# Batched stages of a recurrent-attention layer reordered, and two buffers of its chain exchanged

## The chip, the cores and the metric

The kernel runs on one core of a Trainium2 chip. The metric is the device time of one execution in microseconds (us). The engines of a core work side by side, each through its own list of instructions in order: TensorE (PE, matrix products, with the loads of its weights listed as PEld), VectorE (DVE), ScalarE (ACT), GpSimd (POOL) and SyncE (SP, which here issues transfers only). Transfers (DMAs) are issued by SP, ACT and POOL and carried out by 16 DMA engines.

## The reference

Input and output are a sequence of 2048 tokens of 640 features, bf16. Four layers run one after the other, A, B, A, B, each on the normalized result of the one before and added to it. Layer A is the one that the change touches:

```python
mem = mem0                              # 8 rows of 640
for s in range(64):                     # 64 segments of 32 tokens
    h = concat([mem, xs[s]])            # 40 rows
    q, k, v = h @ Wq, h @ Wk, h @ Wv    # 32 heads of 192
    p = softmax(mask(q @ k.T * 192 ** -0.5))
    o = (p @ v) @ Wo
    mem = o[:8]                         # memory of the next segment
    outs.append(o[8:])
x = x + concat(outs)
```

The mask lets the 8 memory rows see all 40 rows; the 32 tokens see the memory and the tokens up to themselves. Since the memory of a segment is made by the segment before it, the 64 segments are a serial chain. Layer B is a linear attention over the whole sequence.

## The kernel before

**The two stages of a layer A.** Each segment has 40 rows. The kernel takes 32 of them through the chain (8 memory rows and the first 24 tokens) and computes the keys and queries of the last 8 tokens of each segment, the border tokens, for all 64 segments in a batch ahead of it. The batched stage is `A_pre` (from L836), the chain `A_chain` (from L1033). Both write out their order of instructions by hand: each engine runs its list in the order of the code, and a step that waits holds up all that is behind it on its engine.

**Rounds and weights.** The 32 heads go in four rounds r of 8 heads. A matrix Wq, Wk or Wv has five pieces of 384 KB for each round. Some pieces stay in SBUF for the whole layer, the others share slots and are streamed again for each segment (`load_slot`, L748). Half of the output weights of two rounds shares one place in the same way (`load_piece`, L797). A streamed load is held back until a named step of PE (table `PACE`, L26, function `release`), and then goes out on SP's queue.

**`A_pre`.** The segments are worked in two halves h of 32. A step (h, r) computes keys and queries of one round for one half: 120 products at L998, evicted in turn by DVE (L94) and ACT (L96) into one of two staging buffers, and stored to `kqb` in DRAM by a transfer on ACT's queue (L1015). In layer 0 the steps alternate over the halves, rounds 3, 2, 1, 0. In layer 2 half 0 runs through rounds 0 to 3, then half 1 through 3 to 0. Each step issues the loads of its own weights (`load_matrix`, L755 or L748), and layer 0 those of the next round too. `first_values` computes the border values of the first eight segments for a round (L257) and stores them to `vb` (L261). In layer 0 the stage also normalizes all rows as tasks between evictions, and lays the output weights out anew in DRAM, `wo_rows`: 32 transfers of 240 KB on SP (`lay_out_wo`, L816), 16 of them after step (0, 1) and 16 after (0, 0). Parts of them are fetched into SBUF (`early_wo`, `late_wo`, L774). The first 32 rows of the chain, `first_rows`, come by a transfer on SP at L1014.

**`A_chain`.** Each segment runs four rounds n = 0 to 3, every other segment in the reverse order of r. A round projects Q, K and V (L1129), computes scores (L1166), applies exp on ACT (L1247), weights the values (L1179), scales the result on ACT (L1209), turns it on DVE (L1350 for rounds 0 and 2, L1358 for 1 and 3) and multiplies with the output weights into `ps_w` (L1237). For each round POOL fetches the border keys and queries (`kqb`, L1098, three buffers, four turns ahead), copies them into place (L1105) and fetches the border values (`Vp<-vb`, L1109).

The border values themselves are made in the chain for a group of eight segments ahead: at the end of each segment one unit is computed from the tokens `tT` (L257, `next_values`), evicted by ACT at the start of the next segment into `vt` (L1276), and stored to `vb` by SP (L261). The tokens of a new group are loaded by POOL (L247) in two halves through one place `xt`, and turned by DVE (L250), in 6 segments of each layer.

**Who shares which place.** `vt` holds the border values on their way to `vb`, and then the turned rows of round 0 in the same segment. `ots` holds the turned tail rows of the segment before (`otb`) on their way to DRAM, then the turned rows of round 1, then `xt`. The tail rows of the segment's first two rounds go to the second half of `vt` at n = 2.

```python
if n == 0:
    rows = self.two_heads(vt).rearrange("p e (c j) -> p e c j", j=64)
```

Of the kernel before, what the change touches and what calls it, by code (L numbers as in the profile page):

```python
# [122 lines left out]
class Kernel:  # L123
# [139 lines left out]
    def kept_tokens(self):  # L263
        return self.under[:, self.ot_at:self.ot_at + 320].rearrange("p (b t) -> p b t", b=self.KC)
# [571 lines left out]
    def A_pre(self, xn_dram, li, load_matrix, piece, wo_mid, wo_end, lay_out_wo, early_wo, x_raw):  # L836
# [11 lines left out]
        vts = [wo_end[:, 2 * VH * i:2 * VH * i + 2 * VH] for i in range(2 * NR)]  # L848
        with ExitStack() as es:
# [14 lines left out]
            def gather(dst, src, h, k, queues=None):  # L864
                xv = src.rearrange("(s t) d -> t s d", t=32)
                for t2 in range(TP):
                    e = queues[t2 % 2] if queues else nc.gpsimd if k % 2 else nc.scalar
                    e.dma_start(out=dst[SH * t2:SH * t2 + SH, :], in_=xv[24 + TP * k + t2, SH * h:SH * h + SH])
# [54 lines left out]
            def all_rows():  # L923
                rows = [slice(P * b, P * b + P) for b in range(self.NB)]
                t = in_turn([norm_tasks(lambda x, q=q: nc.gpsimd.dma_start(out=x[:], in_=x_raw[q, :]),
                                        lambda xn, q=q: nc.gpsimd.dma_start(out=xn_dram[q, :], in_=xn[:]))
                             for q in rows])
                return [f for i in range(0, len(t), 4) for f in (*t[i:i + 4], None)]

            def keep_tokens(k):  # L930
                nc.gpsimd.tensor_copy(out=self.kept_tokens().rearrange("p b (t s) -> p b t s", s=8),
                                      in_=columns(0).rearrange("p b (t s) -> p b t s", s=SH)[:, :, :, 8 * k:8 * k + 8])

            def first_values(r):
                for G in range(2):
                    ps = ps_.tile([P, 512], F32, name="ps_pre", tag="bank")
                    self.tail_values(ps, lambda i: self.kept_tokens()[:, i, :], r, G, piece)
# [20 lines left out]
            if x_raw is not None:  # L958
# [3 lines left out]
            seen = set()  # L962
            for h, ri, r in steps:
                if h not in seen and (x_raw is None or h == 0):
                    seen.add(h)
                    xBT = columns(h)
                    for k in range(NT):
                        if x_raw is not None:
                            xb = normed[h, k]
                        else:  # L970
                            xb = xB[h][k % 2]
                            gather(xb, xn_dram, h, k)
                        transpose_rows(xb, h, k)
                        if x_raw is not None:
                            busy(3)
                xBT = columns(h)
                if turn == 0:
                    keep_tokens(0)
                st = sts[turn % 2]
                turn += 1  # L980
                if h == 0 and ri == 1:
                    self.build_A_consts()
                if x_raw is not None and (h, ri) == (0, 0):
                    for h1 in range(1, NH):
                        tasks += tails(h1)
                if x_raw is not None and (h, ri) == (NH - 1, 0):
                    tasks += all_rows()
                if x_raw is not None and h == NH - 1 and ri == NR - 1:
                    early_wo(True)
                for mi, m in enumerate("KQ"):  # L990
                    load_matrix(m, r)
# [24 lines left out]
                if x_raw is not None and (h, ri) == (0, 0):  # L1016
                    for h1 in range(1, NH):
                        for k1 in range(NT):
                            transpose_rows(normed[h1, k1], h1, k1)
                if h == 0:  # L1020
                    first_values(r)
                if h == 0 and ri == NR - 1:
                    keep_tokens(1)
                if h == NH - 1 and ri == 1 and x_raw is None:
                    load_matrix("V", 0)
                    early_wo(True)
                if h == NH - 1 and ri == NR - 1:
                    early_wo(False)
# [4 lines left out]
    def A_chain(self, xn_dram, at_dram, li, load_slot, piece, late_wo, load_both, wo, low):  # L1033
# [3 lines left out]
        with tc.tile_pool(name=f"A{li}_ch", reuse_waits="tile", bufs=1) as sp, \  # L1037
# [264 lines left out]
            for s in range(NSEG):  # L1302
# [64 lines left out]
                for n in range(L):  # L1367
# [36 lines left out]
                    if n == 1:  # L1404
                        turn_tails(s, 1)
# [127 lines left out]
```

## Time and profile before

| | us |
|---|---|
| median of 3 runs | 3296.66 |
| lowest and highest | 3291.12, 3306.54 |
| the profiled execution | 3315.67 |
| its span from first to last instruction | 3313.9 |
| PE busy in it | 3038.2 |
| granted TensorE clock in it | 0.987 |

Stages of the profiled execution, from the starts and ends of instructions in its timeline:

| stage | from | to |
|---|---|---|
| layer 0, batched stage | 0 | 157.7 |
| layer 0, first segment of the chain | 157.7 | 199.6 |
| layer 2, batched stage | 1687.7 | 1812.7 |
| layer 2, first segment of the chain | 1812.7 | 1840.9 |

Rows are read like this. A group or timeline row names the line of the kernel, the engine, the operation, and out<-in by the program's names; `x20` counts instructions. `[0.64 <-DVE under L1350]` is idle time of that engine just before, and what ended it. A waits row reads: engine, what waited, what it waited for, then the total in us, the number of times and the longest. A row of the chain of waits has start, duration and what was running or under way. `under` is the SBUF tensor in which `vt`, `ots` and others lie, `arena` the large one with weights. SPq is a transfer issued by SP.

### The profile page before, as it was taken

The page shows a single profiled execution, that of the slowest core. Times are in us where ns is not written, and L with a number is a line of the kernel's source. Part 1 is how long each engine was busy: PE and PEld are TensorE (multiplying, and loading weights), DVE is VectorE, ACT ScalarE, POOL GpSimd, SP SyncE. Part 2 cuts the span into 40 slices and gives each one's busy share as a digit, 9 for nine tenths or more (in the row PEclk, how much of TensorE's full clock was granted, in tenths as well). Part 3 has the DMA queues.
Part 4 walks back from the last instruction along what each step waited for, and adds up shares of the span by engine and source line. Part 5 has one row for each costly group of instructions (what it writes and reads, how often), then busy time and mean ns, then how long its engine had stood idle before and what let it go on. Part 6 is the DMA issues. An engine that isn't in the chain of part 4 may idle for free.

```text
span 3313.9 us, 141368 instructions
## 1 busy us (share of the span) xinstructions
PE 3038.2 (92%) x59586; PEld 1926.3 (58%) x59586; DVE 2170.0 (65%) x5425; ACT 1897.0 (57%) x4537; POOL 1379.5 (42%) x2852
## 2 busy tenths in 40 slices
PE   7879999999999999999999899999999999998999
PEld 5745565565555555555468555565556655555553
DVE  4557677777767667746653676667766766776565
ACT  2346666666666666646443566666666666665463
POOL 1244544545444545431121554545454554454300
PEclk8989999999999999999999999999999999999999
DMA  9787777777777777760277777777777777777400
GB/s 342 276 284 250 232 246 250 244 238 254 247 230 239 248 249 230 253 236 9 94 256 257 260 254 238 232 237 250 249 233 244 254 241 231 247 257 262 164 1 32
DMA packets 338812, 749.66 MB, mean 226 GB/s; under 512 B 68538, under 2 KB 115378, under 8 KB 335106
## 3 DMA queue, kind: packets, MB, share of 16 engines
q1 hardware_dynamic: 268258, 637.09, 56.6%
q0 software_dynamic: 66848, 77.71, 8.7%
q10 hardware_dynamic: 3072, 25.82, 2.0%
q8 instruction: 469, 7.68, 0.9%
q14 instruction: 165, 1.35, 0.1%
HBM read 670.77 MB, written 78.01 MB: 226 GB/s over the span
## 4 chain that ended last, share of the span: by engine, by line
PE 48%; DMA 35%; DVE 7%; ACT 5%; issue 4%; SPq 1%; POOL 0%; DVEq 0%; POOLq 0%; ACTq 0%
DMA vb<-under 12%; DMA arena<-in_A_Wv_dram 11%; PE ps_w L1237 9%; PE ps_qk_k L1129 6%; PE ps_v L1129 6%; PE ps_qk_q L1129 5%; DMA Vp<-vb 3%; PE ps_s L1166 3%; PE kv L1488 2%; PE ps_x L257 2%; PE ps_pre L998 2%; PE ps_o L1179 2%; DMA arena<-wo_rows 2%; PE ps_wo L466 2%; PE ps_pq L517 1%
## 5 line engine op out<-in xcount | busy, mean ns | idle before, releaser
L1129 PEld LDWEIGHTS <-hT 128*32 128x32 bf16 x30720 | 795.2, 97 | 511.1 <-DVE hT L1437 77.2
L1149 DVE STREAM_TRANSPOSE QK<-raws 128x512 bf16<-128x512 bf16 (+1 forms) x1152 | 712.4, 634 | 131.3 <-ACT raws L1144 103.9
L1129 PE MATMUL ps_qk_q<-arena,hT 128*32 128x384 bf16 x10240 | 509.3, 327 | 47.7 <-DVE hT L1437 23.8
L1129 PE MATMUL ps_qk_k<-arena,hT 128*32 128x384 bf16 x10240 | 513.6, 328 | 7.9 <-DMA arena<-in_A_Wk_dram 7.1
L1105 POOL COPY QK<-kqb 64x192 bf16<-64x192 bf16 x1024 | 349.6, 341 | 325.1 <-PE ps_s L1166 286.1
L1109 POOL DMA_DIRECT2D Vp<-vb x512 | 258.1, 504 | 537.5 <-PE ps_t L1192 302.3
L1129 PE MATMUL ps_v<-arena,hT 128*32 128x384 bf16 x8192 | 440.1, 327 | 28.2 <-DMA arena<-in_A_Wv_dram 20.7
L1144 ACT ACTIVATE raws<-ps_qk_k 128x512 bf16<-128x512 f32 (+1 forms) x640 | 313.6, 510 | 220.7 <-PE ps_qk_k L1129 218.7
L1209 ACT ACTIVATE raws<-ps_o,under 128x192 bf16<-128x192 f32 x1024 | 373.6, 420 | 111.0 <-DVE under L1203 104.5
L1144 ACT ACTIVATE raws<-ps_qk_q 128x512 bf16<-128x512 f32 x512 | 304.7, 595 | 230.8 <-DVE under L1350 136.6
L1237 PE MATMUL ps_w<-arena,under 128*32 128x320 bf16 x6144 | 307.8, 301 | 77.1 <-DVE under L1350 57.5
L1158 DVE CAST Vp<-ps_v 64x384 bf16<-64x384 f32 x512 | 286.4, 559 | 51.4 <-ACT Vp L1156 36.9
L1098 POOL DMA_DIRECT2D kqb<-kqb x512 | 287.1, 561 | 73.0 <-POOL QK L1105 59.4
L1166 PEld LDWEIGHTS <-QK 128*80 128x80 bf16 x4096 | 195.4, 120 | 158.6 <-issue 157.0
L1156 ACT ACTIVATE Vp<-ps_v 64x384 bf16<-64x384 f32 x512 | 246.4, 481 | 68.3 <-PE ps_v L1129 66.0
L1166 PE MATMUL ps_s<-QK 128*80 128x80 bf16 x4096 | 252.4, 209 | 2.6 <-PE ps_v L1129 0.7
L1094 POOL DMA_DIRECT2D attn<-under x128 | 91.2, 713 | 360.5 <-DVE under L1090 329.5
L1247 ACT ACTIVATE E<-ps_s 80x320 bf16<-80x320 f32 x512 | 217.6, 425 | 29.3 <-PE ps_t L1192 28.5
L1237 PEld LDWEIGHTS <-under 128*32 128x32 bf16 x6144 | 149.7, 96 | 115.9 <-DVE under L1350 70.6
L998 PEld LDWEIGHTS <-arena 128*128 128x128 bf16 x1920 | 190.8, 100 | 43.5 <-issue 10.7
L1276 ACT ACTIVATE under<-ps_x 128x384 bf16<-128x384 f32 x112 | 55.1, 492 | 264.9 <-PE ps_x L257 264.9
L1179 PE MATMUL ps_o<-Vp,E 80*32 80x193 bf16 x4096 | 179.7, 249 | 22.7 <-DMA Vp<-vb 10.8
(165 smaller groups left out, 4378.3 us busy)
## 6 DMA issues: line engine op xcount, KB each, us to landing
arena<-wo_rows SPq DMA_DIRECT2D x560, 320.0 KB, 5.9
arena<-in_A_Wq_dram SPq DMA_DIRECT2D x427, 384.0 KB, 6.1
arena<-in_A_Wk_dram SPq DMA_DIRECT2D x298, 384.0 KB, 6.7
arena<-in_A_Wv_dram SPq DMA_DIRECT2D x290, 384.0 KB, 7.2
kqb<-arena ACTq DMA_DIRECT2D x16, 1536.0 KB, 10.5
kqb<-kqb POOLq DMA_DIRECT2D x512, 48.0 KB, 5.1
Vp<-vb POOLq DMA_DIRECT2D x512, 24.2 KB, 4.5
otb<-under POOLq DMA_DIRECT2D x256, 48.0 KB, 4.9
```

The costliest lines, as they stand in the source:

```text
L998: nc.tensor.matmul(ps[:, T * i:T * i + T], lhsT=w[b][:, P * c:P * c + P], rhs=xBT[:, b, :], start=(b == 0), stop=(b == KC - 1))
L1098: nc.gpsimd.dma_start(out=kqb[:], in_=self.kqb_d[r, :, s, :])
L1105: nc.gpsimd.tensor_copy(out=o, in_=kqb[h, :].rearrange("p (x c q) -> p x c q", c=3, q=16))
L1109: nc.gpsimd.dma_start(out=Vs[n % 2][64:80, :], in_=self.vb_d[s // 8, r].rearrange("g (t s) x f -> s (g t) (x f)", s=8)[s % 8])
L1129: last = nc.tensor.matmul(o, lhsT=hT[:, b, :], rhs=rhs, start=(i == 0), stop=(i == KC - 1), tile_position=(0, 32 * g), skip_group_check=True)
L1144: nc.scalar.activation(out=raw[:, c], in_=ps[:, c], func=ACT.Copy)
L1149: nc.vector.transpose(out=o, in_=i)
L1156: nc.scalar.activation(out=o, in_=i, func=ACT.Copy)
L1158: nc.vector.tensor_copy(out=o, in_=i)
L1166: nc.tensor.matmul(S[0:80, c0:c0 + 80], lhsT=KT[:, 4 * x + c, :], rhs=QT[:, 4 * x + c, :], start=(c % 2 == 0), stop=(c % 2 == 1), skip_gro ...
L1209: nc.scalar.activation(out=out, in_=i, func=ACT.Copy, scale=rc[G])
L1237: step = nc.tensor.matmul(W[q:q + 32, 0:320], lhsT=OT[i // 6][:, i % 6 // 2, 32 * (i % 2):32 * (i % 2) + 32], rhs=rhs, start=(first and i ...
```

## The change

In `A_pre` the loop over steps is replaced by two written-out orders, with the loads of weights in functions of their own. In layer 0 the weights of rounds 3 and 2 are issued first, those of rounds 1 and 0 after the first two steps, then the copies of the output weights with `early_wo(True)` ahead of the last eight, and then `first_rows`. Layer 2 goes round by round too. Both sets of kept tokens are copied at once, the second to a place in `wo_end`. Loads for half 1 in layer 0 go out on POOL only, and the tasks for all rows have no pauses.

In `A_chain` the turned rows of round 0 go to `ots`, those of round 1 to `vt`. The turned tail rows get a tile of their own, `otb`. `kqb` has two buffers, fetched three turns ahead. The two halves of a new group's tokens lie side by side in `ots`: both are loaded at the end of the segment before, and both are turned in round 0.

```diff
-    def kept_tokens(self):
-        return self.under[:, self.ot_at:self.ot_at + 320].rearrange("p (b t) -> p b t", b=self.KC)
+    def kept_tokens(self, k):
+        return (self.later_tokens if k else self.under[:, self.ot_at:self.ot_at + 320]).rearrange("p (b t) -> p b t", b=self.KC)
...
+        self.later_tokens = wo_end[:, 4 * NR * VH:4 * NR * VH + 320]
...
-                return [f for i in range(0, len(t), 4) for f in (*t[i:i + 4], None)]
...
-                steps = [(h, ri, NR - 1 - ri) for ri in range(NR) for h in range(NH)]
...
-                steps = [(h, ri, ri if h == 0 and NH > 1 else NR - 1 - ri) for h in range(NH) for ri in range(NR)]
...
+            def rows_ready(h):
+                for k in range(NT):
+                    if x_raw is not None:
+                        xb = normed[h, k]
+                    else:
+                        xb = xB[h][k % 2]
+                        gather(xb, xn_dram, h, k)
+                    transpose_rows(xb, h, k)
+                    if x_raw is not None and h == 0:
+                        busy(3)
+                if h == 0:
                     keep_tokens(0)
+                    keep_tokens(1)
+
+            def keys_and_queries(h, r):
+                nonlocal turn
                 st = sts[turn % 2]
                 turn += 1
...
-                    load_matrix(m, r)
...
-                if x_raw is not None and h == 0 and ri + 1 < NR:
-                    for m in "KQ":
-                        load_matrix(m, NR - 2 - ri)
-                if h == 0:
-                    load_matrix("V", r)
-                if x_raw is not None and h == 0 and ri >= 2:
-                    lay_out_wo(((0, 2), (1, 3))[ri - 2])
-                if h == NH - 1 and ri == NR - 2:
-                    nc.sync.dma_start(out=self.first_rows(), in_=self.rows_of(0))
                 nc.scalar.dma_start(out=self.kqb_d[r, :, SH * h:SH * h + SH, :], in_=st)
+            def load_round(r):
+                for m in "KQV":
+                    load_matrix(m, r)
+
+            def fetch_first_rows():
+                nc.sync.dma_start(out=self.first_rows(), in_=self.rows_of(0))
+
+            if x_raw is not None:
+                load_round(3)
+                load_round(2)
+                rows_ready(0)
+                tasks += tails(1)
+                keys_and_queries(0, 3)
+                rows_ready(1)
+                tasks += all_rows()
+                keys_and_queries(1, 3)
+                first_values(3)
+                self.build_A_consts()
+                load_round(1)
+                load_round(0)
+                for r in (0, 2, 1):
+                    lay_out_wo([r])
+                early_wo(True)
+                lay_out_wo([3])
+                fetch_first_rows()
+                keys_and_queries(0, 2)
+                keys_and_queries(1, 2)
+                first_values(2)
+                keys_and_queries(0, 1)
+                keys_and_queries(1, 1)
+                first_values(1)
+                keys_and_queries(0, 0)
+                first_values(0)
+                keys_and_queries(1, 0)
+                early_wo(False)
+            else:
+                load_round(0)
+                rows_ready(0)
+                load_round(2)
+                keys_and_queries(0, 0)
+                first_values(0)
+                self.build_A_consts()
+                keys_and_queries(0, 2)
+                rows_ready(1)
+                keys_and_queries(1, 0)
+                load_round(3)
+                load_round(1)
+                early_wo(True)
+                fetch_first_rows()
+                keys_and_queries(1, 2)
+                first_values(2)
+                keys_and_queries(0, 3)
+                keys_and_queries(1, 3)
+                first_values(3)
+                load_round(0)
+                keys_and_queries(0, 1)
+                first_values(1)
+                keys_and_queries(1, 1)
+                early_wo(False)
...
-            xt = ots[:, 192:352]
-            nc.vector.tensor_copy(out=tT[:], in_=self.kept_tokens())
+            xt = [ots[:, 160 * i:160 * i + 160] for i in range(2)]
             hT = sp.tile([P, KC, 32], BF16, name="hT", tag="hT")
             nc.vector.transpose(out=hT[:], in_=self.first_rows().rearrange("p (j b) -> p b j", b=KC))
+            nc.vector.tensor_copy(out=tT[:], in_=self.kept_tokens(1))
...
-                kqb = sp.tile([P, 192], BF16, name="kqb", tag="kqb", bufs=3)
+                kqb = sp.tile([P, 192], BF16, name="kqb", tag="kqb", bufs=2)
...
-            def turn_tail(rows, otb):
-                self.chain_end = [nc.vector.transpose(out=otb, in_=rows)]
-                return otb
+            def turn_tail(rows):
+                otb = sp.tile([P, 192], BF16, name="otb", tag="otb")
+                self.chain_end = [nc.vector.transpose(out=otb[:], in_=rows)]
+                return otb[:]
...
-            def turn_tails(s, half):
+            def turn_tails(s):
                 if new_set(s):
-                    self.turn_tokens(tT[:, :, 32 * half:32 * half + 32], xt)
-
-            def load_tails(s, half):
+                    for half in range(2):
+                        self.turn_tokens(tT[:, :, 32 * half:32 * half + 32], xt[half])
+
+            def load_tails(s):
                 if new_set(s):
-                    self.load_tails(xt, set_of(s)[0], half)
+                    for half in range(2):
+                        self.load_tails(xt[half], set_of(s)[0], half)
...
-                at = NR * s + n + 4
+                at = NR * s + n + 3
...
-                turn_tails(s, 0)
-                load_tails(s, 1)
+                turn_tails(s)
...
-                        if n == 0:
-                            rows = self.two_heads(vt).rearrange("p e (c j) -> p e c j", j=64)
-                        else:
-                            rows = raw_of["K"][:, 0:384].rearrange("p (e c j) -> p e c j", e=2, j=64)
-                        OTs.append([rows[:, G, :, :] for G in range(2)])
-                        nc.vector.transpose(out=rows, in_=osc.rearrange("p (e c j) -> p e c j", e=2, j=64))
+                        rows = (raw_of["K"][:, 0:384] if n else ots).rearrange("p (c j) -> p c j", j=64)
+                        OTs.append([rows[:, 3 * G:3 * G + 3, :] for G in range(2)])
+                        nc.vector.transpose(out=rows, in_=osc.rearrange("p (c j) -> p c j", j=64))
                         return
                     if n == L:
                         OTs.append([KT[:, 3 * G:3 * G + 3, 0:64] for G in range(2)])
                     else:
-                        OTs.append([ots[:, 192 * G:192 * G + 192].rearrange("p (c j) -> p c j", j=64) for G in range(2)])
+                        OTs.append([vt[:, VH * G:VH * G + 192].rearrange("p (c j) -> p c j", j=64) for G in range(2)])
...
-                load_tails(s + 1, 0)
+                load_tails(s + 1)
```

More of the change, by code (lines that the diff above doesn't have):

```diff
@@ L957, in A_pre @@
             turn = 0
-            if x_raw is not None:
-                steps = [(h, ri, NR - 1 - ri) for ri in range(NR) for h in range(NH)]
-            else:
-                steps = [(h, ri, ri if h == 0 and NH > 1 else NR - 1 - ri) for h in range(NH) for ri in range(NR)]
[L962 to L977, printed above, removed]
+            def rows_ready(h):
[9 more added lines that the diff above has]
+                if h == 0:
                     keep_tokens(0)
+                    keep_tokens(1)
+            def keys_and_queries(h, r):
+                nonlocal turn
                 st = sts[turn % 2]
                 turn += 1
[L981 to L989, printed above, removed]
+                xBT = columns(h)
                 for mi, m in enumerate("KQ"):
-                    load_matrix(m, r)
                     w = [piece(m, r, b) for b in range(KC)]
@@ L1015, in A_pre @@
-                nc.scalar.dma_start(out=self.kqb_d[r, :, SH * h:SH * h + SH, :], in_=st)
[L1016 to L1026, printed above, removed]
@@ L1325, in A_chain @@
                     rows = tail_rows(rct, spare_rows())
-                    otb = turn_tail(rows, ots[:, 0:192])
+                    otb = turn_tail(rows)
                     store_rows(s - 1)
@@ L1440, in A_chain @@
                 W_done = W
-            store_tail(turn_tail(tail_rows(rct, spare_rows()), ots[:, 0:192]), NSEG - 1, order[L])
+            store_tail(turn_tail(tail_rows(rct, spare_rows())), NSEG - 1, order[L])
             keep_rows(W_done)
```

23 lines of the change are left out of this document (9 added, 14 removed).

## The prediction

> **What bounds the kernel now.** I read the page first: the shares of the engines, then the chain of waits.
>
> ```profile
> span 3313.9 us, 141368 instructions
> PE 3038.2 (92%) x59586; PEld 1926.3 (58%) x59586; DVE 2170.0 (65%) x5425; ACT 1897.0 (57%) x4537; POOL 1379.5 (42%) x2852
> DMA vb<-under 12%; DMA arena<-in_A_Wv_dram 11%; PE ps_w L1237 9%; PE ps_qk_k L1129 6%; PE ps_v L1129 6%; PE ps_qk_q L1129 5%; DMA Vp<-vb 3%; PE ps_s L1166 3%; PE kv L1488 2%; PE ps_x L257 2%; PE ps_pre L998 2%; PE ps_o L1179 2%; DMA arena<-wo_rows 2%; PE ps_wo L466 2%; PE ps_pq L517 1%
> ```
>
> TensorE (PE) is the bound, with 8% of the span to lose or gain. Two transfers stand at the head of the chain: the store of the border values, `vb<-under`, and the load of the streamed value weights, `Wv`. So I asked next for PE's own waits over the whole span.
>
> ```profile
> PE ps_w L1237 <- DVE under L1350: 57.5, 107, 1.4
> PE ps_v L1129 <- DMA arena<-in_A_Wv_dram: 20.7, 41, 1.2
> PE ps_o L1179 <- DMA Vp<-vb: 10.8, 21, 1.4
> PE ps_v L1129 <- issue: 6.3, 9, 0.9
> ```
>
> The columns are total, times, longest. The largest wait, 57.5 us in 107 segments (0.54 us each), is the one that the swap of places aims at. One segment's chain of waits (span 603 to 626) shows it, and its timeline shows the streamed loads:
>
> ```profile
> 606.19 6.20 DMA vb<-under
> 612.52 0.59 DVE under L1350
> 613.15 0.73 PE ps_w L1237 x16
> 618.68 0.69 issue
> 619.37 0.83 PE ps_v L1129 x15
> 611.15 0.84 SPq L748 DMA_DIRECT2D arena<-in_A_Wv_dram  x2
> ```
>
> The store takes 6.20 us, and DVE's transpose of round 0's rows (L1350) can't write over those bytes before it lands. PE stands until 613.15. Then, 5.5 us later, PE stands again ("issue", 0.69) in the middle of the last value projection, just as the second of the two Wv loads is due.
>
> **The change, part by part.**
>
> *Swap of places in the chain.* Round 0's rows go to `ots`, which no store reads, and round 1's go to `vt`, whose store landed at about 612.4 in this segment, a full round before round 1's own transpose. So the 57.5 us at L1237 go; the instructions stay the same in number and shape. What is late next? The Wv loads were issued at 611.15, released by earlier projections and not by the stalled step. Their landing therefore stays where it is against the segment's start, while PE arrives sooner. That the landing can't simply come sooner too, the windows show:
>
> ```profile
> core 0: us, PE busy (x) PEld busy (x) DVE busy (x) ACT busy (x) POOL busy (x), PEclk, DMA share, GB/s
> 612.00:614.00 2.00, 1.36 (x36) 1.04 (x36) 1.32 (x3) 0.81 (x2) 0.72 (x3) 1.00 0.99 364
> 614.00:616.00 2.00, 2.00 (x64) 1.41 (x56) 1.41 (x4) 1.36 (x5) 0.74 (x2) 1.00 1.04 406
> 618.00:620.00 2.00, 1.31 (x35) 0.56 (x24) 1.59 (x5) 1.25 (x4) 1.07 (x2) 1.00 1.03 365
> 622.00:625.00 3.00, 2.76 (x62) 1.43 (x57) 1.64 (x6) 0.87 (x3) 2.10 (x5) 1.00 0.19 45
> ```
>
> From 612 to 620 the DMA engines are full (the last two columns are their busy share, 0.99 to 1.04 here, and GB/s), and idle again at the end of the segment. The Trainium skill (DMA: Bandwidth & Descriptors, Specifications) gives some 358 GB/s of HBM per core as a limit. The 406 GB/s of a row above lie over that figure, so the rows decide; by the figure too the loads would be at their limit in this stretch, and little of the stall would be kept.
>
> How much is kept: PE waits for Wv already in 41 segments, and with "issue" before the same projection in 9 more, 50 in all. There the whole 0.54 us turns into a longer Wv wait. In the other 57 of 107, at most 57 x 0.54 = 31 us stay as a gain, and at least nothing, depending on how much before PE the load landed. I take the middle, 15 us: the landing has spread in both groups, and no row splits them further. **Term 1: -15 us** (bounds 0 and -57.5).
>
> *Both halves of a set's border tokens loaded at the segment's end and turned at once* (12 segments). POOL no longer waits for DVE between the halves:
>
> ```profile
> POOL under L247 <- DVE tT L250: 14.0, 12, 1.2
> ```
>
> Behind that wait the load `Vp<-vb` was queued, for which PE waits 10.8 us in all (above). Against this, DVE now waits at round 0 for both loads, up to the same 1.2 us in each of 12 segments. Bounds -10.8 and +14; I take 0, as both are of one size.
>
> *Two `kqb` buffers, not three.* Each fetch of the border keys and queries is issued one turn nearer to its use. POOL in the same segment, and the page's row:
>
> ```profile
> 611.48 0.56 POOL L1098 DMA_DIRECT2D kqb<-kqb  x1
> 617.03 0.74 POOL L1105 COPY QK<-kqb 64x192 bf16<-64x192 bf16 x2 [0.72 <-PE ps_s L1166]
> 620.13 0.50 PE L1166 MATMUL ps_s<-QK 128*80 128x80 bf16 x8
> kqb<-kqb POOLq DMA_DIRECT2D x512, 48.0 KB, 5.1
> ```
>
> The nearest pair is a fetch at 611.48 for the copy at 617.03: 5.55 us for a transfer of median 5.1. If it is late, the copy slips; the scores that read it start at 620.13, 2.4 us after the copy's end, so this cover hides it. Without the cover it would cost its lateness in 124 segments, about 0.5 us each, 62 us. I take +1 (bounds 0 and +62, nearest to the row with cover). `otb` in a tile of its own removes a reuse and adds none.
>
> *Layer 0's batched stage.* What PE loses up to the end of the first segment:
>
> ```profile
> 157.74 1.79 PE L1129 MATMUL ps_qk_q<-arena,hT 128*32 128x384 bf16 x20 [12.12 <-DVE ps_qk_q L1065]
> 178.44 0.46 PE L1237 MATMUL ps_w<-arena,under 128*32 128x320 bf16 x4 [12.08 <-DMA arena<-wo_rows]
> 199.62 0.67 PE L1129 MATMUL ps_qk_q<-arena,hT 128*32 128x384 bf16 x12
> 129.91 34.11 SPq L816 DMA_DIRECT2D wo_rows<-in_A_Wo_dram  x16
> SPq L816 <- DMA kqb<-arena: 46.3, 4, 15.2
> PE ps_pre L257 <- DMA arena<-in_A_Wv_dram: 9.4, 5, 4.1
> PE ps_pre L998 <- DVE arena L94: 5.6, 2, 4.9
> 1812.71 1.00 PE L1129 MATMUL ps_qk_q<-arena,hT 128*32 128x384 bf16 x20 [0.58 <-DVE ps_qk_q L1065]
> 1840.86 1.00 PE L1129 MATMUL ps_qk_q<-arena,hT 128*32 128x384 bf16 x20
> ```
>
> The first segment takes 199.62 - 157.74 = 41.9 us, layer 2's 1840.86 - 1812.71 = 28.2. The difference is the output weights: the second half of their copies goes out from 129.91 to 164, held on SP by `kqb` stores (46.3 us, four waits), and the 12.08 us at 178.44 follow. Now all 32 copies stand ahead of the last three rounds. Is there bandwidth for it? A full stretch, and all that the DMA engines moved to 178 us:
>
> ```profile
> 40.00:60.00 20.00, 15.07 (x129) 12.60 (x126) 4.09 (x11) 3.72 (x8) 3.21 (x5) 0.93 1.04 385
> DMA packets 22606, 55.70 MB, mean 313 GB/s; under 512 B 4270, under 2 KB 10882, under 8 KB 21567
> ```
>
> At the 385 GB/s of the full stretch above, 55.70 MB take 145 us, less than the 157.74 at which the chain starts. So the 12.08 us go: **term 2: -12 us** (bounds 0 and -14, the difference to layer 2). In the stage itself the wait for the first Wv pieces (9.4) goes, as first values come after two rounds of keys, and so does most of L94's 5.6, since half 1's rows are turned at another place. In exchange the `kqb` stores on ACT now meet SP's long queue. Before, SP waited up to 15.2 us for such a store; if ACT waits in its turn for SP's copies, its evictions are queued behind it, and PE for them. And `first_rows` is behind the 32 copies, so the chain's start may slip by the time that they run late. I set these against the 15 us gained: 0 (bounds -15, and +30 for two waits of 15.2).
>
> *Layer 2's batched stage.* There PE waits for Wk and around the second half's rows, and the first segment for early output weights:
>
> ```profile
> PE ps_pre L998 <- DVE next_xT L94: 2.6, 1, 2.6
> PE ps_pre L998 <- DMA arena<-in_A_Wk_dram: 2.4, 4, 0.7
> PE ps_pre L998 <- DVE arena L94: 1.6, 1, 1.6
> ```
>
> Going over both halves with one set of weights halves what must stream between rounds, so the 2.4 us go, and early output weights a round sooner cut some of the first segment's excess. **Term 3: -4 us** (bounds +5, one more wait at a round's start, and -6.6, all three).
>
> **Sum:** -15 + 0 + 1 - 12 + 0 - 4 = -30 us. The profiled execution took 3315.67 us (span 3313.9 and 1.8 around it), so 3285.7; the median of the runs shown is 3296.66, 19 us or 0.6% lower, and the same sum from there gives 3266.7. I forecast 3266 us.
>
> **Rivals.**
>
> *A: the stall is kept whole.* Then Wv must land sooner as well. The last segments of the chain, which have no border values to store, speak for it:
>
> ```profile
> 1360.42 1.00 PE L1129 MATMUL ps_qk_q<-arena,hT 128*32 128x384 bf16 x20 [1.07 <-DVE hT L1437]
> 1372.49 0.98 PE L1129 MATMUL ps_v<-arena,hT 128*32 128x384 bf16 x20
> ```
>
> There the last projection runs 12.07 us after the first without a wait. Against it: those segments also have no 97 KB store among the loads, which the changed kernel keeps. Time: 57.5 + 12 + 4 = 73 us, 3223.
>
> *B: the stall moves whole, and layer 0 gives its 12 us back as a later chain start.* For it: the full windows, and `first_rows` behind all copies. Against it: 57 segments had no Wv wait. Time: -4 to +1, 3296 at the likeliest; the swap then does nothing that PE can use.
>
> *C, slower: shared completion slots between ACT's and SP's transfers.* The 46.3 us in which SP's copies waited for `kqb` stores show that the two queues are tied. With all copies ahead, the tie turns round: each of the last five stores on ACT waits for copies still in SP's queue, ACT's evictions stop, and PE starves. It decides once the waits of ACT beyond PE's eight accumulators exceed the 30 us of the sum; five waits of 10.5 us (the store's landing on the page, below) are 52, so +22: 3319. Against it: the copies have 158 us to run in, and DVE takes half the evictions.
>
> ```profile
> kqb<-arena ACTq DMA_DIRECT2D x16, 1536.0 KB, 10.5
> ```
>
> The Trainium skill (DMA: Bandwidth & Descriptors, Queues, rings and completion order) has a transfer's count land only after every earlier write of that DMA engine, across its queues; that would lengthen just these waits. No run here shows it yet.
>
> **How the numbers follow.** About 0.5%, 16.5 us, is what a measurement of this kernel can tell from no change. Forecast (-20 to -45) 0.50; A 0.16; B 0.21; C, with the uncovered `kqb` fetch, 0.13. Faster: forecast and A, 0.66; same: B, 0.21; slower 0.13. The range goes from 3226, with about half of A below it, to 3302, which is B's +1 and some drift of the median over 3297; C and a tail of B lie above. That leaves out about 0.2. The forecast's own is 3250 to 3278.
>
> **What would show it.** Step 1: no PE wait at L1237 for the transpose of round 0, and Wv waits before `ps_v` grown from 27 us to about 70; if they stay near 27, A holds. Step 2: all L816 copies issued before the chain's start, and the first segment near 29 us; the chain's start within 4 us of 157.74. C shows as idle of ACT's evictions behind a `kqb` store and of PE behind L96. A late fetch shows as POOL's copy waiting for `kqb` and PE's scores for POOL. The forecast is wrong if the segments of a chain shorten by over 0.4 us each, or grow, or if layer 0's chain starts after 165.

## The result, and the profile after

The changed kernel takes 3270.6 us (median of 10 runs, 3262.0 to 3286.1), the kernel before 3301.1 beside it (10 runs). The ratio is 0.9912, 95% interval 0.9891 to 0.9933: 22 to 36 us faster, about 29 in the middle. The profiled execution took 3279.9 us, its span 3278.1.

The page of the changed kernel, the span, the engines and the chain of waits:

```profile
span 3278.1 us, 141616 instructions
PE 3043.7 (93%) x59586; PEld 1930.3 (59%) x59586; DVE 2157.5 (66%) x5425; ACT 1901.7 (58%) x4537; POOL 1384.0 (42%) x2856
DMA arena<-in_A_Wv_dram 17%; PE ps_qk_q L1154 9%; PE ps_w L1263 9%; PE ps_v L1154 9%; PE ps_qk_k L1154 8%; PE ps_pre L985 5%; PE ps_s L1191 4%; PE kv L1510 2%; DMA vb<-under 2%; PE ps_o L1204 2%; DVE raws L1457 2%; PE ps_wo L466 2%; DMA Vp<-vb 2%; DMA arena<-in_A_Wk_dram 1%; PE ps_pq L517 1%
```

The store of the border values fell from 12% of the chain to 2%, and the loads of Wv rose from 11% to 17%. PE's waits over the whole span (total, times, longest) say the same. ("issue" is idle time for which the profile names no cause.) Line numbers have moved: L1154 is the projection (L1129 before), L1263 the output product (L1237), L1374 the transpose (L1350).

```profile
PE ps_v L1154 <- DMA arena<-in_A_Wv_dram: 35.1, 65, 1.7
PE ps_w L1263 <- issue: 27.1, 41, 1.7
PE ps_qk_q L1154 <- DVE ps_qk_q L1090: 18.8, 2, 18.3
PE ps_v L1154 <- issue: 7.2, 14, 1.3
```

The 57.5 us at the output product for the transpose of round 0 are not in the list any more. One segment's chain of waits (span 500 to 520) shows what the path runs through instead:

```profile
506.37 0.37 PE ps_qk_q L1154 x9
506.74 7.47 DMA arena<-in_A_Wv_dram
514.21 0.04 issue
514.25 0.35 PE ps_v L1154 x4
```

A Wv load takes 7.47 us, and PE resumes as it lands. Before, a store of 6.20 us stood at this place in the chain.

By stages, from the ends of the segments (the end of DVE's sums `hT`, with which the next segment can start) and the first and last product of the batched stages, in the two profiled executions:

| stage | before, us | after, us | difference |
|---|---|---|---|
| layer 0, up to the end of the first segment | 199.6 | 188.2 | -11.4 |
| layer 0, the other 62 full segments | 1198.6 | 1190.5 | -8.1 |
| layer 2, products of the batched stage | 124.2 | 115.5 | -8.7 |
| layer 2, from there to the end of the first segment | 28.9 | 29.8 | +0.9 |
| layer 2, the other 62 segments | 1200.7 | 1193.2 | -7.5 |

By this pair alone the two chains gave 16 us. But a chain moves by more than that with nothing changed: the new chain's 124 segments took 2383.7 us here and up to 2411.6 in the profiles of the runs below, and the old chain's 2399.4 here and 2401.1 behind the new batched stages, within that range. Layer 0's first stage and layer 2's batched stage repeat within 3 us.

### The profile page after: what moved, and what is told of

Same layout as the page of the kernel before. It is cut to its first block, busy times and chain, and to the rows that moved or that the text cites. A ratio compares the mean times of both kernels' runs of the same rounds, so it can differ in the third digit from the quotient of the medians.

```text
span 3278.1 us, 141616 instructions
## 1 busy us (share of the span) xinstructions
PE 3043.7 (93%) x59586; PEld 1930.3 (59%) x59586; DVE 2157.5 (66%) x5425; ACT 1901.7 (58%) x4537; POOL 1384.0 (42%) x2856
## 4 chain that ended last, share of the span: by engine, by line
PE 60%; DMA 25%; DVE 7%; issue 3%; ACT 3%; POOL 0%; SPq 0%; POOLq 0%; DVEq 0%; ACTq 0%
DMA arena<-in_A_Wv_dram 17%; PE ps_qk_q L1154 9%; PE ps_w L1263 9%; PE ps_v L1154 9%; PE ps_qk_k L1154 8%; PE ps_pre L985 5%; PE ps_s L1191 4%; PE kv L1510 2%; DMA vb<-under 2%; PE ps_o L1204 2%; DVE raws L1457 2%; PE ps_wo L466 2%; DMA Vp<-vb 2%; DMA arena<-in_A_Wk_dram 1%; PE ps_pq L517 1%
## 5 line engine op out<-in xcount | busy, mean ns | idle before, releaser
L1154 PEld LDWEIGHTS <-hT 128*32 128x32 bf16 x30720 | 801.6, 97 | 540.8 <-issue 98.0
L1154 PE MATMUL ps_qk_q<-arena,hT 128*32 128x384 bf16 x10240 | 512.0, 328 | 54.1 <-DVE hT L1459 25.5
L1130 POOL COPY QK<-kqb 64x192 bf16<-64x192 bf16 x1024 | 351.9, 344 | 456.7 <-DMA kqb<-kqb 205.6
L1154 PE MATMUL ps_qk_k<-arena,hT 128*32 128x384 bf16 x10240 | 515.7, 328 | 6.4 <-DMA arena<-in_A_Wk_dram 3.8
L1154 PE MATMUL ps_v<-arena,hT 128*32 128x384 bf16 x8192 | 447.0, 328 | 43.0 <-DMA arena<-in_A_Wv_dram 35.1
L1263 PE MATMUL ps_w<-arena,under 128*32 128x320 bf16 x6144 | 310.0, 301 | 14.4 <-issue 11.8
L1263 PEld LDWEIGHTS <-under 128*32 128x32 bf16 x6144 | 149.5, 96 | 45.2 <-issue 19.9
```

Source lines behind the costliest of these rows:

```text
L1130: nc.gpsimd.tensor_copy(out=o, in_=kqb[h, :].rearrange("p (x c q) -> p x c q", c=3, q=16))
L1154: last = nc.tensor.matmul(o, lhsT=hT[:, b, :], rhs=rhs, start=(i == 0), stop=(i == KC - 1), tile_position=(0, 32 * g), skip_group_check=True)
L1263: step = nc.tensor.matmul(W[q:q + 32, 0:320], lhsT=OT[i // 6][:, i % 6 // 2, 32 * (i % 2):32 * (i % 2) + 32], rhs=rhs, start=(first and i ...
```

## The experiments

Every ratio is that to the kernel before, run beside it on the same chip. The median of before was 3313 to 3320 us there.

### The chain and the batched stages, one at a time

The first kernel has the new `A_chain` behind the old `A_pre`, the second the reverse. Besides that only the place of the kept tokens is fitted: the first diff is against the new chain, the second against the old one.

```diff
-            nc.vector.tensor_copy(out=tT[:], in_=self.kept_tokens(1))
+            nc.vector.tensor_copy(out=tT[:], in_=self.kept_tokens())
```

```diff
-            nc.vector.tensor_copy(out=tT[:], in_=self.kept_tokens())
+            nc.vector.tensor_copy(out=tT[:], in_=self.kept_tokens(1))
```

> The chain of the changed kernel behind the batched stages of before. My theory: the swap removes the waits for the transpose of round 0 (57.5 us), and all but about 15 us come back as waits for streamed weights, so some 15 us faster than before (ratio 0.995), with the ps_w waits for that transpose gone and waits for Wv and 'issue' about 30 us larger. Rival A (the whole stall is kept): ratio 0.983. Rival B (the swap does nothing, the gain is all in the batched stages): ratio 1.000.

> The batched stages of the changed kernel ahead of the chain of before. My theory: layer 0 gives 11 us up to the end of the first segment and layer 2's batched stage 8 us, about 19 us together (ratio 0.994), and this run and the one with the chain alone add up to the changed kernel's 0.991. If the swap carried all of it, ratio 1.000; if the batched stages did, 0.991.

The chain alone: 0.9992 (0.9977 to 1.0007), nothing that can be told from no change. The batched stages alone: 0.9940 (0.9926 to 0.9953), 20 us. PE's waits with the new chain alone:

```profile
PE ps_v L1129 <- DMA arena<-in_A_Wv_dram: 44.0, 74, 1.2
PE ps_w L1238 <- issue: 24.0, 34, 1.8
PE ps_qk_k L1129 <- DMA arena<-in_A_Wk_dram: 16.8, 31, 1.1
PE ps_o L1179 <- issue: 10.0, 10, 1.7
```

Set against the waits with the old chain (Wv 20.7 and "issue" of the output product 17.0 in the first profile), Wv has grown by 23 us, "issue" of the output product by 7, and Wk and `ps_o` by some 10 and 8. The wait for the store was removed, and most of its 57.5 us came back at four other places. (The profiled execution took 3324 us, 9 over the median of its kernel.) That is rival B in the chain, not my term of -15. The new chain holds more than the swap: two `kqb` buffers, `otb` and the tails are in it, and no run has the swap without them.

The changed kernel was run once more beside others:

> The changed kernel unaltered, beside kernels that share its runs of before. The chain alone measured 0.9992 and the batched stages alone 0.9940; if the chain gives nothing beside them either, 0.993 to 0.994 is to be seen here; if the swap gives some 15 us once the stages are changed too, 0.989 to 0.991.

It measured 0.9933 (0.9908 to 0.9959), which is the two parts put together (0.9992 x 0.9940 = 0.9932). The first measurement, 0.9912, overlaps with it. Over both, the batched stages give 20 us, and the chain between nothing and some 10.

### Is it the streamed weights that take the stall's place?

Two pairs of kernels stream less in each segment, on either side of the change. In the first pair only Wv is short, in the second all streamed weights.

```diff
+        def load_short(m, r, b):
+            holds[m, b] = r
+            self.last_load = nc.sync.dma_start(out=slot[m, b][:, 0:96], in_=wview[m][:, b, PW * r:PW * r + 96])
+            return self.last_load
...
-                        self.held.append(lambda b=b: load_slot(m, order[NR - 1], b))
+                        self.held.append(lambda b=b: self.load_short(m, order[NR - 1], b))
...
-            self.last_load = nc.sync.dma_start(out=into[:, c:c + 1280], in_=self.wo_rows[r, :, own + c:own + c + 1280])
+            self.last_load = nc.sync.dma_start(out=into[:, c:c + 96], in_=self.wo_rows[r, :, own + c:own + c + 96])
```

(In the first pair `load_short` is used for V alone, and the output pieces stay whole.)

> The kernel before with the streamed Wv loads of the chain cut to 96 of 1536 columns (the rest of their slots keeps older values, so part of the value projections is computed from other weights). It takes 0.72 MB of some 4.7 MB per segment away. Theory: the waits for Wv (27 us with 'issue') vanish and the waits for the transpose of round 0 stay near 50 us or shrink with a faster store; some 25 to 40 us faster than before.

> The changed kernel with the same cut of the streamed Wv loads. Theory (the swap's gain is eaten by streamed weights): with the loads short the swap is worth 40 us or more against the short version of before, beside the 20 us of the batched stages: 60 us or more between the two. Rival (the swap only moves the wait to something else, PE's own order or the other engines): the two differ by the 20 to 30 us that the kernels differ by with full loads.

> The kernel before with all streamed loads of the chain (Q, K, V and the output pieces) cut to 96 columns (the rest keeps older values, so part of the projections is computed from other weights). Theory: the waits for weights vanish, the waits for the transpose of round 0 stay unless the store lands sooner with the DMA engines free: with the store at 3 us in place of 6.2 they vanish too, and then this kernel is as fast as the changed one with the same cut.

> The changed kernel with the same cut of all streamed loads. Theory (the DMA engines' load is at the root of both waits): with little streamed neither kernel waits for the store, and the two differ by the 22 us of the batched stages alone. Rival (the store is slow by itself): before still waits some 40 to 57 us for the store, and the two differ by 60 to 80 us.

| streamed | before, us | changed, us | difference | less the batched stages (20 to 22) |
|---|---|---|---|---|
| all, whole | 3319.9 | 3297.1 | 23 | about 0 |
| Wv short | 3244.2 | 3190.0 | 54 | about 33 |
| all short | 3133.2 | 3111.9 | 21 | about 0 |

The middle row shows that the new chain does have a worth, about 33 us, as soon as Wv is out of the way; even the nearest ends of the intervals of the two ratios (0.9740 to 0.9794 and 0.9592 to 0.9641) lie 33 us apart, over the 20 of the batched stages. I had asked for 40 or more. I had also expected 25 to 40 us of the cut of Wv in the kernel before, and it brought 76: beside the waits for Wv themselves, "issue" at the output product fell from 17.0 to 4.1 us and the waits for `Vp`, 10.8 before, went. The Wv loads held up more than the waits that bear their name. With Wv short, before still waits for the store (first row, kernel before), and the changed kernel waits for the weights that are left (the other two):

```profile
PE ps_w L1244 <- DVE under L1357: 52.0, 104, 0.9
```

```profile
PE ps_qk_k L1161 <- DMA arena<-in_A_Wk_dram: 13.8, 29, 1.1
PE ps_w L1270 <- issue: 13.4, 21, 1.9
```

The last row of the table shows that both waits come from the streamed loads. With nearly nothing streamed, the kernel before has no wait for the store either, although its transpose of round 0 still goes to the bytes that the store reads. The waits of that line in the kernel before, first whole (span 600 to 1000), then with all loads short:

```profile
L1350 DVE STREAM_TRANSPOSE under<-raws x20: 579/579/580, 612.5 to 981.6; 128x384 bf16<-128x384 bf16 x20
...
  DMA vb<-under: 16.6, 20
```

```profile
L1357 DVE STREAM_TRANSPOSE under<-raws x22: 565/566/580, 617.4 to 995.5; 128x384 bf16<-128x384 bf16 x22
...
  ACT raws L1216: 1.0, 4
```

In 20 of 20 segments DVE waited for `vb<-under`; with short loads in none of 22. The traces' records of single packets agree: the last of the store's 128 packets ends 5.15 us after its issue with whole loads, 5.14 with Wv short and 3.91 with all short (medians of 53 segments). The segments are 18.00 us then, in both kernels to 0.01, and 19.2 to 19.5 with whole loads. Windows of 200 us (600 to 800) of the kernel before, whole and short; the first pair after the span is PE's busy time, the last two columns the share of the DMA engines and GB/s:

```profile
600.00:800.00 200.00, 186.66 (x4418) 118.81 (x4414) 139.46 (x357) 125.57 (x311) 100.23 (x210) 1.00 0.74 241
```

```profile
600.00:800.00 200.00, 197.25 (x4746) 127.58 (x4749) 149.38 (x381) 134.98 (x333) 107.47 (x226) 1.00 0.24 52
```

These are means over whole segments. Inside the segment that the prediction shows, the engines are full from 612 to 620, when the Wv loads are under way, but not yet while the store is, from 606.19 to 612.39:

```profile
605.40:608.00 2.60, 2.60 (x68) 1.71 (x72) 1.65 (x6) 2.41 (x6) 0.64 (x1) 1.00 0.47 133
608.00:610.00 2.00, 1.99 (x48) 1.23 (x44) 1.74 (x4) 1.40 (x3) 1.28 (x4) 1.00 0.85 225
610.00:612.00 2.00, 2.00 (x60) 1.22 (x48) 1.07 (x3) 1.57 (x4) 1.08 (x3) 1.00 0.78 180
```

Loads of Wq go out on SP's queue just ahead of the store and just behind it (605.76 and 606.78). So it is shown that streamed loads lengthen the store, but not whether by the bandwidth that they take or by their place on the same queue; no run issues the store on another one. The swap removed the wait for the store and left the full stretch behind it as it was.

### Releasing the weights sooner

If the loads are merely issued late, sooner releases should help, as the DMA engines are half idle at a segment's start.

```diff
-PACE = {("Q", 0): 0, ("K", 0): 1, ("V", 0): 3, ("Q", 1): 4, ("K", 1): 4, ("V", 1): 3, ("Q", 2): 1, ("K", 2): 0, ("V", 2): 0,
-        ("Q", 3): 0, ("K", 3): 0}
+PACE = {("Q", 0): (0, 3), ("K", 0): (1, 4), ("V", 0): (1, 4), ("Q", 1): (2,), ("K", 2): (0,), ("V", 2): (0,),
+        ("Q", 3): (0,), ("K", 3): (0,)}
...
-                    if PACE.get((m, n)) == i:
+                    if i in PACE.get((m, n), ()):
```

> The changed kernel with the streamed weights released up to 3 us sooner in each segment (the two pieces of Wv after the steps V0 and Q1 in place of V1 and Q2; those of Q and K sooner in step; the output pieces as before). Theory: PE's waits in the chain are for loads that are issued too late, in a stretch where the DMA engines are full, while they are half idle at the segment's start; so the Wv waits (35 to 45 us) fall under 15 and the kernel is 15 to 30 us faster than the changed one. Rival (the loads are bound by the bytes of a segment, or the sooner loads push back the kqb and Vp fetches): the waits move to ps_o, ps_s or the output weights and the time stays within 5 us.

It measured 0.9947 (0.9924 to 0.9970), not faster than the changed kernel's 0.9933 beside it. PE's waits with sooner releases (the profiled execution, 3321 us, was the slowest of twelve; their median is 3302, that of the changed kernel 3297):

```profile
PE ps_v L1154 <- DMA arena<-in_A_Wv_dram: 31.0, 49, 1.1
PE ps_o L1204 <- DMA Vp<-vb: 19.4, 13, 2.9
PE ps_v L1154 <- issue: 14.8, 19, 2.0
PE ps_qk_k L1154 <- issue: 11.4, 11, 2.9
```

In the unaltered kernel run beside it Wv stood at 41.7 and `Vp<-vb` at 11.7. The wait moved again, to the fetch of border values and to the keys. The rival held.

### Two `kqb` buffers

```diff
-                kqb = sp.tile([P, 192], BF16, name="kqb", tag="kqb", bufs=3)
+                kqb = sp.tile([P, 192], BF16, name="kqb", tag="kqb", bufs=2)
...
-                at = NR * s + n + 4
+                at = NR * s + n + 3
```

> The kernel before with two kqb buffers and fetches three turns ahead, and nothing else changed. The chain alone measured 0.9992, so either the swap gives nothing (my present theory: all of it comes back as waits for streamed weights) or it gives some 15 us that the two buffers lose again. Theory: ratio 1.000 to 1.001. Rival (late fetches): 1.004 to 1.006, with PE waiting in ps_s for POOL's copies.

Measured 0.9973 (0.9958 to 0.9989): some 9 us faster, which neither theory said. POOL's waits show that the fetches do land late for its copies, a wait that isn't among those of over 52 us in the kernel before:

```profile
POOL QK L1105 <- DMA kqb<-kqb: 145.1, 127, 3.8
```

PE has no wait of any size behind it, so the cover that I named (scores well after the copy) holds. Why the kernel gets faster is open; PE's waits in its profile (54.9 us for the transpose of round 0, 20.0 for Wv) are close to those of before. What it excludes is that late fetches ate the swap's gain: in the changed kernel, too, POOL waits 205.6 us for `kqb` and PE only 2.9 us for POOL's copies. If the 9 us hold in the new chain, then the swap with the tails and `otb` cost some 6 us there (-3 for the whole chain); no run shows it.

### Layer 0: what sets the chain's start

In the changed kernel PE ends the batched stage near 142 us and stands 18.3 us. The chain of waits there:

```profile
142.74 8.16 DMA kqb<-arena
150.91 0.55 SPq L816
...
153.53 4.45 DMA under<-xn
158.00 0.07 DVE hT L1081
...
160.21 1.79 PE ps_qk_q L1154 x19
```

SP's last copies (L816) wait for the last `kqb` store on ACT's queue, 8.16 us, and the first rows (`under<-xn`) are behind the copies on SP. The copies do not read that store. But the trace has both queues take turns on eight semaphores (101 and 110 to 116) that count a transfer's end, the completion slots: the store and the fifth of these eight copies have the same one, 113, and the copy goes out only when the store has landed. In layer 0 SP waited so for `kqb` stores six times before (68.2 us) and four times in the changed kernel (39.7 us). Two edits take the two links apart, and one kernel has both:

```diff
+                fetch_first_rows()
                 early_wo(True)
                 lay_out_wo([3])
-                fetch_first_rows()
```

```diff
-                nc.scalar.dma_start(out=self.kqb_d[r, :, SH * h:SH * h + SH, :], in_=st)
+                q = nc.gpsimd if x_raw is not None and r == 0 else nc.scalar
+                q.dma_start(out=self.kqb_d[r, :, SH * h:SH * h + SH, :], in_=st)
```

> The changed kernel with the transfer of the first rows issued ahead of early_wo(True) and the last eight copies. In the changed kernel PE stands 18.3 us before the chain, since the first rows wait behind copies that wait for a kqb store. Theory (the order on SP sets the chain's start): the chain starts near 145 instead of 160, some of it is lost again to output weights that come later, and the kernel is 5 to 12 us faster than the changed one (3260). Rival (layer 0 is bound by the bytes to be moved): the end of the first segment stays at 188 and the time at 3270.

> The changed kernel with the two kqb stores of layer 0's last round issued by POOL, so that they share no completion slot with SP's copies. Theory (SP's last copies wait for the kqb stores on ACT): the last copies are out by about 140, the first rows land near 145, the chain starts near 148, some 5 to 10 us faster than the changed kernel. Rival (the copies are late because the DMA engines are full): the chain still starts near 158 and the time stays at 3270, or grows by POOL's own time for issuing the two stores.

> The changed kernel with both edits of layer 0: the first rows fetched ahead of early_wo(True) and of the last eight copies, and the last round's kqb stores issued by POOL. With the one the first segment ended at 183.7, with the other at 181.1, with neither at 185.6 to 188.2. Theory (SP's order and the shared slots are two causes): the chain starts near 143, the first segment ends near 176, 10 us sooner than in the changed kernel, ratio 0.990. Rival (the bytes bound it): it ends at 181 and the ratio is 0.993.

| kernel | chain starts | first segment ends | ratio |
|---|---|---|---|
| changed, two profiles | 160.2, 157.8 | 188.2, 185.6 | 0.9912, 0.9933 |
| rows first | 142.3 | 183.7 | 0.9935 (0.9919 to 0.9951) |
| `kqb` on POOL | 149.4 | 181.1 | 0.9931 (0.9916 to 0.9947) |
| both | 141.7 | 178.1 | 0.9905 (0.9886 to 0.9924) |

With rows first the chain starts 18 us sooner, as expected, and gives most of it back. First PE waits 6.21 us for POOL's copy of border keys, which stands on POOL behind a fetch (`Vp<-vb`) that waits for the store of the border values, then 5.01 us for output weights:

```profile
150.67 1.08 POOL L1134 DMA_DIRECT2D Vp<-vb  x2 [7.21 <-DMA vb<-arena]
152.15 1.09 PE L1191 MATMUL ps_s<-QK 128*80 128x80 bf16 x8 [6.21 <-POOL QK L1130]
163.15 0.46 PE L1263 MATMUL ps_w<-arena,under 128*32 128x320 bf16 x4 [5.01 <-DMA arena<-wo_rows]
```

With both edits the wait for output weights is gone, and that for POOL's copy is there again with 5.25 us, behind 6.56 us in which POOL waits for the border values. The first segment ends 7 to 10 us sooner than in the changed kernel. I had said 176, and 178 was measured. Each edit alone ends the stage some 2 to 7 us sooner, too little to show in a ratio; neither brought the 5 us and more that I had expected of it. Both together are the fastest ratio measured with the whole computation, though its interval overlaps with those of the changed kernel, and it was not run beside it.

## Why the prediction was right, and where it was not

The time forecast, 3266, lies 5 us from the measured 3271, and the -30 of the sum from the -29 measured. Part of that is compensation: one term was too large and another too small. Part is luck: the two parts measured by themselves give -20 and -3, and the second measurement of the changed kernel -22, 7 or 8 us short of the sum.

*Term 1, -15 for the swap: mis-sized.* The direction of the mechanism was right. The waits for the transpose of round 0 vanished, the Wv waits grew, and the loads landed as late as before (median 7.0 us after issue, 7.2 before). But I priced the return at Wv alone and took the middle of 0 and 31. The chain by itself measured -3 us (interval -8 to +2): the time that did not return at Wv returned at the output product ("issue", which goes with all loads short), Wk and `ps_o`. The step that failed is the sentence that in the other 57 segments the stall might stay as a gain: it asked only whether the *next* load was late, while all of them came through the same full stretch (0.99 to 1.04 busy in the prediction's windows from 612 to 620). The lower bound, nothing, was the better value. My test for the step, Wv waits grown from 27 to about 70, was met by a third to a half (42 in the first profile, 49 with the chain alone). Rival A, the whole stall kept, is refuted by the chain alone.

*`kqb`, +1: wrong in sign*, -9 alone, with the cause open. The term's reason (the copy slips, the scores don't) was seen. The tails' 0 was not tried by itself.

*Term 2, -12 for layer 0: right in size.* The first segment's end moved by 11.4 us in the first pair of profiles. The first segment shrank from 41.9 to 28.0 us, as the output weights were laid out before it, and the 12.08 us of waiting went. The batched stage itself came out 2.5 us later by its chain start, within what I set as 0: PE was through sooner, and then stood for the first rows. Here rival C was partly there: the tie of ACT's stores and SP's copies cost the start of the chain some 8 us, mostly not by stopping ACT's evictions, as I had it, but through SP and the first rows. It did stop them as well:

```profile
ACT arena L96 <- DMA arena<-in_A_Wk_dram: 7.0, 2, 5.4
ACT ln_lv L289 <- DMA arena<-in_A_Wk_dram: 9.3, 1, 9.3
```

ACT waited for SP's loads 16.3 us in three waits. The two long ones, 9.3 and 5.4, lie at `kqb` stores whose completion slot a load of Wk still held, which is what rival C describes. DVE's and PE's slack took most of it: PE waited 5.2 us for L96 up to 200 us, 1.60 and 2.05 of it behind these two.

*Term 3, -4 for layer 2: too small.* The products of the stage took 115.5 in place of 124.2 us, beyond my bound of -6.6. The four Wk waits went as predicted, and of the 2.4 us of waits around the second half's rows 1.40 stayed. The first segment, of which I had hoped for a part, came out 0.9 us longer. Some 1.5 us of the gain are chance: the stage's first step took 16.08 us before and 14.55 after, and 13.27 to 16.12 in the other profiles of the new order. What I left out is what a wait does to the products behind it. Timeline rows of a step of 120 products before, undisturbed and after the Wk waits, and windows over the latter (the third number from the right is the granted clock):

```profile
1720.40 13.27 PE L998 MATMUL ps_pre<-next_xT,arena 128*128 128x256 bf16 x120
...
1737.92 0.40 PE L998 MATMUL ps_pre<-next_xT,arena 128*128 128x256 bf16 x1 [0.74 <-DMA arena<-in_A_Wk_dram]
1739.04 15.57 PE L998 MATMUL ps_pre<-next_xT,arena 128*128 128x256 bf16 x116 [0.72 <-DMA arena<-in_A_Wk_dram]
```

```profile
1735.00:1737.85 2.85, 1.20 (x9) 0.33 (x5) 0.21 (x1) 0.00 (x0) 0.00 (x0) 1.00 1.05 405
1737.85:1744.67 6.82, 6.03 (x28) 4.12 (x29) 0.69 (x1) 1.09 (x2) 0.80 (x1) 0.50 1.05 398
1744.67:1754.60 9.93, 9.93 (x93) 8.71 (x93) 3.58 (x5) 2.68 (x4) 0.80 (x1) 1.00 0.66 239
```

116 products take 15.57 us after the waits where 120 take 13.27 otherwise, and the granted clock was 0.50 from 1737.85 to 1744.67. So 2.4 us of waiting cost about 2.7 us more behind them (15.57 less 116/120 of 13.27), which fits the 5.63 us at half the clock from 1739.04 to 1744.67: half of them is 2.8. It was no chance: in the profiles of all five kernels with the old order of layer 2 the clock falls to half at these waits, and the step takes 18.5 to 22.2 us from its first product to its last; in the nine with the new order no step behind the first takes more than 13.3. In the changed kernel the step that uses the second set of weights runs at full speed:

```profile
1685.05 13.27 PE L985 MATMUL ps_pre<-next_xT,arena 128*128 128x256 bf16 x120
```

The Trainium skill (TensorE: Matmul & The Clock Gate, HAM oscillation — how this bites in real kernels) gives as the rule that TensorE shall have no idle gaps of over some 3.4 us. In this trace the longest of the four gaps was 0.74 us (their rows give 0.29, 0.69, 0.74 and 0.72), and the clock fell all the same. Single gaps of 1.58 us in the same stage before (at 1770.49) and 1.40 us after (at 1700.28) were not followed by a lower clock.

## What to carry to other kernels

Where a wait ends with a transfer, look at how full the DMA engines are in the stretch behind it before pricing its removal; if they are full there, another transfer is the next to be late, and the gain of moving a buffer can be nothing. Streaming less on both sides of a change tells in a pair or two of runs whether a wait hangs on the dependence alone or on the loads beside it. And price a stall of TensorE with the products behind it, by comparing a step after a stall with an undisturbed one.

## What the runs showed that I had not expected

Four waits of Wk, 2.4 us in all within 3.4 us, halved the granted clock for 6.8 us, and doubled their own cost.

A store of 97 KB that took 6.20 us beside whole weight loads cost no wait at all with the loads cut, without a change to its order or its place.

Fewer buffers for the small fetches made the kernel before 9 us faster, though POOL then waited 145 us for them.
